# The first group's lists and the first expert block moved ahead, and five later steps that change places, in an attention and mixture-of-experts kernel

## The chip, the cores and the metric

The kernel runs on one core of one Trainium2 chip. The metric is the device time of one execution in microseconds (us). The engines are TensorE (PE, with its weight loads as PEld), VectorE (DVE), ScalarE (ACT), GpSimd (POOL) and SyncE (SP). Each runs its own instructions in the order in which they are written. They meet only at semaphores, and all large loads and transpositions are DMAs that SP issues.

## The reference

Linear attention with positive random features, and a mixture of experts with one expert for each token on its result:

```
def phi(x):
    proj = np.einsum('bhsd,md->bhsm', x, omega)
    sq = np.sum(x * x, axis=-1, keepdims=True) / 2.0
    h = proj - sq
    h = h - np.max(h, axis=-1, keepdims=True)
    return np.exp(h) / np.sqrt(m)
q_p, k_p = phi(q * scale), phi(k * scale)
kv = np.einsum('bhsm,bhsd->bhmd', k_p, v);  z = np.sum(k_p, axis=2)
num = np.einsum('bhsm,bhmd->bhsd', q_p, kv)
den = np.einsum('bhsm,bhm->bhs', q_p, z)[..., None] + 1e-06
x = num / den                      # 8 batches, 8 heads, 576 tokens, 64 wide
...
logits = x @ w_gate                # 4608 tokens, 512 wide, 8 experts
e_idx = np.argmax(logits, axis=1)
...
for e in range(E):
    mask = e_idx == e
    h = np.maximum(x[mask] @ w1[e], 0.0)
    ye = h @ w2[e]
    out[mask] = gate_w[mask, None] * eom[mask, e, None] * ye
```

All of it is in float32; the kernel splits operands into a float16 high half and a float16 low half and adds products.

## The kernel before

The attention is cut into 32 units u (one head of two batches, 1152 positions of keys and of queries). The 32 units make four groups of eight units, and after each group the tokens of its two batches are routed: a chain of small DVE instructions finds expert and place of each token, and lists which tokens make up the blocks of 128 rows of one expert. Each block n is then worked: its rows are gathered, transposed, multiplied with the first weights (two halves, hA and hB), passed through relu, and multiplied with the second weights (out.n.0 and out.n.1). Blocks of one group run among the units of the next.

The order of all of this is one hand-written table of words, ORDER. Plan.order walks through it, and every word emits its instructions on its own engine, so that the table sets the order on each of the five engines. A second table, BANKS, gives each step that needs PSUM one of eight banks; a step that takes a bank waits until the step that had it before is done with it. A third, FILL, says how many matmuls of 512 columns each of six steps warm.0 to warm.5 issues; their results are thrown away. The words that matter here (for the halves of a unit, n = 2u is the key, n = 2u+1 the query):

- pp.u.g (L681, PE): projections of a third g of unit u, into one bank for the key and one for the query, 18 matmuls which alternate between the two; mx.n.g (L699, DVE) takes the extremum of one bank, nb.u.g (L706, L710, DVE) makes the bias of both, and ex.n.g (L716, ACT, three exponentials) empties one bank.
- eh.n (L737, ACT) and el.n (L739, POOL): the high and the low half of the exponentials of n; eT.u (L781, SP): the transposition of the query's halves by DMA; pn.u.0 and pn.u.5 (L867, L874, PE) read its result; xf.u (L881 to L885, DVE) divides.
- kv.u.0 and kv.u.1 (L804, from unit 12 on L798, PE): the sums of key features times values; then one after another kvs.u (L824, DVE), kt.u (L840, PE), ke.u (L849, ACT), kg.u (L846, PE), gh.u (L852, ACT) and gl.u (L855, DVE), which releases the bank of kv.
- lists.g, pid.g, gi.g, controls.g: the end of a group's routing. lists.g (L1172 to L1183, DVE) feeds pid.g (L1306, PE), and that gi.g (L1313, L1339, DVE), the addresses for the gathers gx.n (L1584, POOL). xt.n (L1595, SP) transposes what gx.n gathered.
- w0h and w0l (L521 on ACT, L526 on DVE): halves of the first expert's weights; sw.n.1 and sw.n.2: on ACT and DVE, a branch that splits new weights if block n has another expert than the one before. hA.n and hB.n (L1618, PE) wait for xt.n and for sw.n.1 on both engines; relu.n (L1625, ACT) and rest.n (L1629, DVE) follow; out.n (L1651, PE) waits for rest.n and sw.n.2; os.n (L1694, ACT) and put.n (POOL) write the result.
- lga.u (L920, POOL) adds unit u's part of the gates' logits; lo.u (L591, POOL) makes the low half of unit u's input.

A gather gx.n in this table carries a mark such as gx.0<9: it also waits until the transposition eT.9 has landed.

Of the kernel before, what the change touches and what calls it, by code (L numbers as in the profile page):

```python
# [113 lines left out]
bounded.0 eh.21 gl.9 xf.8.0 mx.22.0 advance.0:0 ld.t.13 xf.8.5:0 pp.11.1 flag.0.1.ACT+DVE mx.23.0 w0h.2.3 advance.0:1 mx.22.1 pn.9.5 xf.9.5:0 w0h.2.2
advance.0:2 gx.2<9 xt.0 mx.23.1 nb.11.0:0 kv.10.0 el.21 xf.8.5:1 nb.11.1:0 advance.0:3 xf.9.5:1 nb.11.0 w0h.1.3 nb.11.1 advance.0:4 kv.10.1 ex.22.1
ld.t.14 xf.8.5 eT.10 kvh.10 advance.0:5 xf.9.5 w0l.1.3 pn.9.0 kvs.10 xf.9.0:0 w0l.1.2 flag.0.1.SP ex.23.0 pp.11.2 ex.23.1 xf.9.0:1 bring.0.1 ex.22.0
kt.10 advance.0:6 sw.0.1 hi.13.0 pp.12.0 xf.9.0 bring.1.1 advance.0:7 mx.24.0 w0h.2.1 advance.0:8 lo.13.0 warm.3 hA.0 mx.22.2 ke.10 sqr.12 w0h.2.0
mx.25.0 mx.23.2 relu.0.0 advance.0:9 nb.12.0:0 nb.11.2:0 kg.10 advance.0:10 nb.12.0 nb.11.2 ld.v.12 lga.8 w0l.2.1 gx.1<9 hB.0 gh.10 gl.10 rest.0.0
ex.22.2 ex.23.2 w0l.2.2 w0l.2.3 sqa.13 relu.0.1 kv.11.0 ex.24.0 pp.12.1 advance.0 kv.11.1 pp.12.2 w0l.2.0 bring.0.2 sw.0.2 eh.23 mx.24.1 out.0.0
ex.25.0 sw.1.1 el.23 mx.24.2 ld.t.15 xh.8 mx.25.1 nb.12.1:0 ld.n.15 hi.14.0 bring.2.1 kvh.11 pn.10.5 nb.12.1 mx.25.2 ld.n.14 vh.12 ld.v.13 xt.1 eT.11  # L120
rest.0.1 bring.1.2 nb.12.2:0 xl.8 ex.25.1 xf.10.5:0 ex.24.1 nb.12.2 sqr.13 vl.12 out.0.1 pn.10.0 ex.24.2 ex.25.2 xf.10.5:1 sqa.14 xf.10.5 pp.13.0
eh.24 os.0 lo.14.0 kvs.11 sw.1.2 mx.26.0 hA.1 eh.25 kt.11 mx.27.0 ke.11 pp.13.1 ld.v.14 xf.10.0:0 xf.10.0:1 nb.13.0:0 relu.1.0 hB.1 el.24 sqr.14
xf.10.0 kg.11 nb.13.0 xh.9 mx.26.1 ex.26.0 rest.1.0 ld.n.16 mx.27.1 kv.12.0 nb.13.1:0 el.25 nb.13.1 ex.27.0 sw.2.1 sqa.15 pp.13.2 ld.t.16 mx.26.2
ex.27.1 mx.27.2 nb.13.2:0 out.1.0 gh.11 xt.2 eT.12 ex.26.1 relu.1.1 vh.13 gl.11 nb.13.2 pp.14.0 ld.n.17 bring.2.2 ex.27.2 rest.1.1 ex.26.2 sqr.15
mx.28.0 kv.12.1 sqa.16 kvh.12 eh.26 mx.29.0 hi.15.0 lga.9 kvs.12 pn.11.0 pp.14.1 mx.28.1 out.1.1 nb.14.0:0 eh.27 nb.14.0 gx.3<11 xl.9 vl.13 mx.29.1
nb.14.1:0 ex.28.0 put.0<11 bring.3.1 kt.12 el.26 xf.11.0:0 os.1 hA.2 xh.10 rows.4 sqr.16 ex.29.0 nb.14.1 pn.11.5 ex.29.1 xt.3 pp.14.2 ex.28.1 kv.13.0
xf.11.5:0 sw.2.2 ke.12 mx.28.2 lga.10 xf.11.0:1 xf.11.5:1 kg.12 hi.16.0 hB.2 xf.11.5 mx.29.2 gh.12 sw.3.1 nb.14.2:0 gl.12 lo.15.0 nb.14.2 relu.2.0
ld.v.15 ex.28.2 ld.n.18 pn.12.5 ex.29.2 rest.2.0 kv.13.1 relu.2.1 ld.t.17 vh.14 kvh.13 pn.12.0 pp.15.0 el.27 eh.28 kvs.13 eT.13 kt.13 sqa.17 vh.15
xl.10 hA.3 xf.12.5:0 gx.4<12 mx.30.0 ke.13 mx.31.0 kg.13 vl.14 xf.11.0 sqr.17 gh.13 xf.12.0:0 xf.12.0:1 xf.12.5:1 gl.13 xh.11 eh.29 xf.12.0 out.2.0
# [1660 lines left out]
```

## Time and profile before

| | |
|---|---|
| median of 3 runs | 623.45 us (618.49 to 624.92) |
| the profiled execution | 623.36 us, its span 621.6 us |
| PE busy | 587.6 us, 95% of the span |
| ACT busy, DVE busy, POOL busy | 413.9, 408.0, 361.2 us |
| mean granted TensorE clock | 0.996 of full speed |

How to read it: PE is busy nearly all the time, so that in most places a microsecond counts only if PE waits in it. Busy time does not tell useful work from thrown-away work (warm) and does not tell where PE waits; both are read from the timeline of one engine, where a merged row gives start, length, engine, line, operation and operands, the number of instructions, and in brackets how long the engine stood idle before and who released it.

### The profile page before, as it was taken

What the parts mean: (1) busy time and instruction counts of PE and PEld (TensorE: products, weight loads), DVE (VectorE), ACT (ScalarE), POOL (GpSimd) and SP (SyncE); (2) the same over time, 40 slices, a digit from 0 to 9 for tenths busy, and PEclk for the clock granted to TensorE, in tenths of its full rate; (3) what the DMA queues carried; (4) which work ended last, traced back from release to release, by engine and by line L of the source; (5) the groups of instructions that cost most, each with busy time, mean ns of one, the idle gap of its engine ahead of it and who ended that gap; (6) DMA issues with size and microseconds to landing.
All of it is one profiled execution on the core that took longest, in us unless ns stands there. A gap on an engine that the chain in (4) does not pass through costs nothing. (4 is left out here: it accounts for less than half of the span.)

```text
span 621.6 us, 21399 instructions
## 1 busy us (share of the span) xinstructions
PE 587.6 (95%) x8442; PEld 451.1 (73%) x8442; DVE 408.0 (66%) x1114; ACT 413.9 (67%) x971; POOL 361.2 (58%) x265
## 2 busy tenths in 40 slices
...
GB/s 296 274 291 293 314 269 195 246 268 246 346 208 247 213 215 263 194 197 245 285 236 247 145 203 204 150 227 221 184 147 338 93 91 132 295 65 91 109 289 33
DMA packets 144686, 133.74 MB, mean 215 GB/s; under 512 B 104606, under 2 KB 124448, under 8 KB 143264
## 3 DMA queue, kind: packets, MB, share of 16 engines
...
q8 instruction: 82, 1.34, 0.9%
q14 instruction: 60, 0.49, 0.3%
...
## 5 line engine op out<-in xcount | busy, mean ns | idle before, releaser
L716 ACT ACTIVATE ef<-pp,nb 128x128 f32<-128x128 f32 x576 | 164.6, 393 | 40.2 <-DVE nb L710 29.6
L699 DVE TENSOR_REDUCE pp<-pp 128x3 f32<-128x384 f32 x192 | 106.7, 562 | 46.6 <-PE pp L681 40.6
L739 POOL TENSOR_TENSOR es<-ef,es 128x1152 f16<-128x1152 f32 x44 | 104.5, 2378 | 38.4 <-ACT es L737 21.7
L1618 PE MATMUL ph<-xt,w1h 128*128 128x128 f16 (+1 forms) x2048 | 122.2, 217 | 1.0 <-issue 0.6
L1618 PEld LDWEIGHTS <-w1h 128*128 128x128 f16 x2048 | 113.5, 98 | 6.9 <-issue 1.7
L1584 POOL DMA_INDIRECT gx<-rows,gi x38 | 41.0, 1079 | 130.1 <-ACTq L1551 63.3
L1629 DVE SCALAR_TENSOR_TENSOR hl<-ph,hh 128x512 f16<-128x512 f32 (+1 forms) x76 | 50.6, 666 | 99.7 <-ACTq L1551 73.8
L1651 PEld LDWEIGHTS <-hh 128*128 128x128 f16 x560 | 51.5, 98 | 54.5 <-issue 0.8
L1625 ACT ACTIVATE hh<-ph 128x512 f16<-128x512 f32 (+1 forms) x76 | 44.7, 591 | 65.6 <-PE ph L1618 50.9
L1618 PE MATMUL ph<-xt,w1l 128*128 128x128 f16 (+1 forms) x1024 | 66.7, 218 | 2.3 <-issue 2.3
L591 POOL TENSOR_TENSOR xlo<-xt,xhi 128x1152 f16<-128x1152 f32 x24 | 57.2, 2381 | 11.2 <-ACT xhi L588 11.1
L1651 PE MATMUL po<-w2h,hh 128*128 128x512 f16 x240 | 62.6, 383 | 0.0
L1651 PE MATMUL po<-w2h,hl 128*128 128x512 f16 x240 | 62.3, 382 | 0.0
L1651 PE MATMUL po<-w2l,hh 128*128 128x512 f16 x240 | 61.6, 379 | 0.0
L1694 ACT ACTIVATE os<-po,gx 128x512 f32<-128x512 f32 (+1 forms) x35 | 24.2, 692 | 54.9 <-PE po L1651 45.6
L1618 PEld LDWEIGHTS <-w1l 128*128 128x128 f16 x1024 | 58.5, 98 | 2.8 <-issue 2.8
L737 ACT CAST es<-ef 128x1152 f16<-128x1152 f32 x44 | 51.6, 1178 | 4.4 <-DMA et<-es 3.5
L1651 PEld LDWEIGHTS <-hl 128*128 128x128 f16 x280 | 27.5, 99 | 33.9 <-issue 1.1
L907 POOL TENSOR_TENSOR xs<-xf,xs 128x576 f16<-128x576 f32 x32 | 40.9, 1281 | 17.4 <-DVE nb L710 6.6
L867 PE MATMUL pn<-kvs,et 128*128 128x81 f16 x768 | 39.9, 201 | 3.1 <-DMA et<-es 1.2
L867 PEld LDWEIGHTS <-et 128*128 128x128 f16 x768 | 34.3, 97 | 8.7 <-issue 3.1
L681 PEld LDWEIGHTS <-xhi 64*128 64x128 f16 x864 | 25.6, 94 | 15.7 <-issue 9.0
...
## 6 DMA issues: line engine op xcount, KB each, us to landing
...
```

What stands on the lines that cost most here:

```text
L591: plan.add(("lo", u, x), ("POOL",), lambda t0=t0, t1=t1: nc.gpsimd.tensor_tensor(out=xl(u)[:, t0:t1], in0=xt32(u)[:, t0:t1], in1=xh(u)[:, ...
L699: nc.vector.tensor_reduce(out=spare(g, 0)[:, i], in_=banks["pp", 2 * u + i, g][:, 0:3, :], op=ALU.min, axis=AX.X)
L716: nc.scalar.activation(ef(2 * u + i)[:, c, :], banks["pp", 2 * u + i, g][:, c % 3, :], AF.Exp, bias=nb(u)[:, i, c : c + 1], scale=-SK)
L737: nc.scalar.copy(es(slot_es(n))[:, 0], ef(n))
L739: nc.gpsimd.tensor_tensor(out=es(slot_es(n))[:, 1], in0=ef(n), in1=es(slot_es(n))[:, 0], op=ALU.subtract)
L867: nc.tensor.matmul(pn[:, c - c0, :], a[:, c, :], w[:, :, 0 if c < 4 else 1], start=(i == 0 and c == c0), stop=(c == NC - 1 and i == len(op ...
L907: nc.gpsimd.tensor_tensor(out=x[:, :, P + o : P + o + D], in0=xf(u)[:, :, 0:D], in1=x[:, :, o : o + D], op=ALU.subtract)
L1584: return nc.gpsimd.indirect_dma_start(out=gx(n), out_offset=None, in_=rows[0 : (j + 1) * NC * P], in_offset=bass.IndirectOffsetOnAxis(ap=t ...
L1618: nc.tensor.matmul(ph[:, f4, 0:w_], w[qd][:, kk, fo : fo + P], xt(n)[:, x, 0:w_], start=(z == 0 and f4 == 0 and x == 0), stop=(z == 1 and ...
L1625: nc.scalar.activation(hh(n)[:, sl, 0:w_], banks["ph", n, g][:, :, 0:w_], AF.Relu)
L1629: nc.vector.scalar_tensor_tensor(out=hl(n)[:, sl, 0:w_], in0=banks["ph", n, g][:, :, 0:w_], scalar=0.0, in1=hh(n)[:, sl, 0:w_], op0=ALU.ma ...
L1651: nc.tensor.matmul(po, x(n)[:, f, :], w[f // 2][:, f % 2, :], start=(f == 0 and a == 0), stop=(f == FC - 1 and a == 2))
```

## The change

No arithmetic is added or removed, but for four matmuls of FILL whose results nobody reads: warm.2 goes from 8 to 7 and warm.3 from 4 to 1. Everything else is order:

1. Around the first group's routing (units 8 to 13): lists.0, pid.0, gi.0 and the gather gx.0 go ahead of mx.21.2 and of the bias of unit 10's last third; mx.20.2 goes behind lists.0, and four links of controls.0 go behind gi.0. On POOL gx.0 goes ahead of lo.12.0, on SP xt.0 ahead of two loads (ld.v.11, ld.t.13). On PE pid.0 goes ahead of pn.8.0 and warm.5, warm.3 ahead of pn.9.0, and hA.0 ahead of kt.10 and pp.12.0. On ACT w0h.1.3 goes ahead of two others, ex.22.0 ahead of four steps, and ex.21.1 and ex.21.2 swap. On DVE sw.0.1 goes ahead of one link of advance.0. Three banks of PSUM change hands: warm.5, pid.0 and pn.8.5.
2. On ACT eh.41 goes behind relu.9.0, ex.43.1 and ex.43.2; on POOL el.41 behind vl.21.
3. On ACT eh.48 goes behind ex.49.2 and ex.49.1.
4. On PE kv.24.0 goes behind hB.14.
5. On ACT ex.53.1 goes ahead of os.14.
6. On POOL el.63 goes ahead of lga.29.

The core of the diff (one line of the first region, one of the second edit, and the end of FILL; the other lines are words of the table in another order):

```
-pn.8.5 kg.9 ex.21.2 ex.21.1 gi.0:0 pp.11.0 lo.12.0 controls.0:3 ld.v.10 xf.8.0:0 gi.0 ex.20.2 ld.v.11 controls.0 xf.8.0:1 w0l.1.0 gh.9 gx.0<9
...
+lists.0:0 ke.9 lists.0:1 warm.2 sqa.12 lists.0 pid.0 mx.20.2 gi.0:0 gi.0 gx.0<9 lo.12.0 mx.21.2 nb.10.2:0 gl.8 pn.8.0 warm.5 controls.0:0 nb.10.2
...
+xf.9.0:1 bring.0.1 sw.0.1 hA.0 kt.10 advance.0:6 hi.13.0 pp.12.0 xf.9.0 bring.1.1 advance.0:7 mx.24.0 w0h.2.1 advance.0:8 lo.13.0 mx.22.2 ke.10 sqr.12
...
-relu.9.0 el.41 pn.19.0 kvh.20 vl.21 ex.43.1 rest.9.0 ex.43.2 pp.22.0 kvs.20 xf.19.0:0 sw.10.1 ex.42.2 eh.42 mx.44.0 relu.9.1 kt.20 el.42 advance.1:4
...
-FILL = (5, 6, 8, 4, 4, 3,)
+FILL = (5, 6, 7, 1, 4, 3,)
```

Three places of it, engine by engine. First PE around the first block, before (kv_2049 is unit 10's bank, pp_0_2179 and pp_0_2180 those of pp.12.0, ph_0 that of hA.0, ph_1 that of hB.0; of runs that alternate one row stands for each kind):

```order
L681 MATMUL pp_2_2127<-omh,xlo_1830 128x128
...
L840 MATMUL kv_2049<-cmt,kvs_2078 128x128
L681 MATMUL pp_0_2179<-omh,xhi_1823 128x128
...
L681 MATMUL pp_0_2180<-omh,xlo_1949 128x128
L479 MATMUL fill_2219<-omh 128x512
L1618 MATMUL ph_0_2224<-xt_2044,w1h_85 128x128
...
L846 MATMUL kv_2049<-wgh,kvf_2274 128x32
L1618 MATMUL ph_1_2300<-xt_2044,w1h_87 128x128
```

And now:

```order
L681 MATMUL pp_2_2131<-omh,xlo_1830 128x128
...
L1618 MATMUL ph_0_2175<-xt_2040,w1h_85 128x128
...
L840 MATMUL kv_2049<-cmt,kvs_2080 128x128
L681 MATMUL pp_0_2229<-omh,xhi_1823 128x128
...
L681 MATMUL pp_0_2230<-omh,xlo_1876 128x128
L846 MATMUL kv_2049<-wgh,kvf_2270 128x32
L1618 MATMUL ph_1_2296<-xt_2040,w1h_87 128x128
```

The first half of the first block now stands directly behind pp.11.2, and unit 10's kt and the whole of pp.12.0 stand behind it; the filling matmuls are gone from here.

Second DVE at the end of the first group's routing, before (r_itc is what lists.0 makes, pid what PE made of it, gi the addresses, pp_2 the banks of unit 10's last third, w1l a low half of weights):

```order
L699 TENSOR_REDUCE pp_2_1802<-pp_2_1802 128x3
...
L1079 TENSOR_TENSOR place<-cmt,rt_1605 128x1152
...
L699 TENSOR_REDUCE pp_2_1802<-pp_2_1803 128x3
...
L1183 TENSOR_TENSOR r_itc<-r_eq,rt_1605 128x18x8
L526 SCALAR_TENSOR_TENSOR w1l_90<-r_101,w1h_86 128x1024
L1313 TENSOR_REDUCE pid_1895<-pid_1895 128x8
...
L1339 CAST gi_1957<-pid_1895 128x8
```

And now:

```order
L1079 TENSOR_TENSOR place<-cmt,rt_1605 128x1152
...
L1183 TENSOR_TENSOR r_itc<-r_eq,rt_1605 128x18x8
L699 TENSOR_REDUCE pp_2_1802<-pp_2_1802 128x3
L1313 TENSOR_REDUCE pid_1860<-pid_1860 128x8
L1339 CAST gi_1872<-pid_1860 128x8
L699 TENSOR_REDUCE pp_2_1802<-pp_2_1803 128x3
...
L526 SCALAR_TENSOR_TENSOR w1l_90<-r_101,w1h_86 128x1024
```

One reduction alone stands now between lists.0 and the two links that wait for PE's answer, where a reduction's bias, controls and a split of weights stood.

Third POOL at the end of the attention, before (es_10433 is unit 31's query, lga the sum of logits, xs the rows that unit 29 writes):

```order
L1584 DMA gx_10448<-rows,gi_8234 128x528
...
L920 TENSOR_TENSOR lga_8995<-lga_8995,xf_10230 128x144
L739 TENSOR_TENSOR es_10433<-ef_10061,es_10433 128x1152
L907 TENSOR_TENSOR xs_10193<-xf_10230,xs_10193 128x9x64
```

And now:

```order
L1584 DMA gx_10444<-rows,gi_8230 128x528
...
L739 TENSOR_TENSOR es_10429<-ef_10057,es_10429 128x1152
L920 TENSOR_TENSOR lga_8991<-lga_8991,xf_10226 128x144
L907 TENSOR_TENSOR xs_10189<-xf_10226,xs_10189 128x9x64
```

The low half of unit 31 no longer stands behind a sum that waits for unit 29's division.

## Rows read from the trace of the kernel before

**Rows 1.** Busy time by stretch: stretch, its length, each engine, clock, DMA, GB/s.

```profile
100.00:150.00 50.00, 48.26 (x778) 38.66 (x777) 41.88 (x117) 47.55 (x117) 35.09 (x23) 1.00 1.02 255
```

**Rows 2.** Timeline of PE around the first block.

```profile
108.30 0.27 PE L840 MATMUL kv<-cmt,kvs 128*128 128x128 f16 x2 [0.60 <-DVE den L881]
...
108.91 0.36 PE L681 MATMUL pp<-omh,xlo 64*128 64x128 f16 x6
109.39 1.02 PE L479 MATMUL fill<-omh 128*128 128x512 f16 x4
110.47 1.95 PE L1618 MATMUL ph<-xt,w1h 128*128 128x128 f16 x32
...
113.15 0.18 PE L846 MATMUL kv<-wgh,kvf 128*128 128x32 f16 x1
...
115.90 1.34 PE L804 MATMUL kv<-rawv,ef 128*128 128x130 f32 x10
```

**Rows 3.** Timeline of DVE there.

```profile
105.51 0.20 DVE L710 SCALAR_TENSOR_TENSOR nb<-pp,sqs 128x6 f32<-128x6 f32 x2
...
110.34 0.56 DVE L699 TENSOR_REDUCE pp<-pp 128x3 f32<-128x384 f32 x1
...
115.14 0.20 DVE L855 SCALAR_TENSOR_TENSOR kvs<-kv,kvs 128x32 f16<-128x32 f32 x1
```

**Rows 4.** Timeline of ACT there.

```profile
109.54 1.15 ACT L588 CAST xhi<-xt 128x1152 f16<-128x1152 f32 x1 [0.20 <-ACTq L1546]
```

**Rows 5.** Timeline of POOL there.

```profile
101.23 2.03 POOL L1584 DMA_INDIRECT gx<-rows,gi  x1 [2.10 <-DVE den L883]
```

**Rows 6.** Timeline of DVE in the third group's routing, two links of one chain.

```profile
339.12 0.24 DVE L1137 TENSOR_TENSOR rt<-cft,rt 128x72 f32<-128x72 f32 x1
339.39 0.23 DVE L1139 TENSOR_TENSOR r_within<-rt,r_avs 128x72 f32<-128x72 f32 x1
```

**Rows 7.** Timeline of ACT at unit 20's query.

```profile
256.06 1.15 ACT L737 CAST es<-ef 128x1152 f16<-128x1152 f32 x1 [1.92 <-DMA et<-es]
```

**Rows 8.** Timeline of PE at the same place.

```profile
258.54 0.21 PE L681 MATMUL pp<-omh,xhi 64*128 64x128 f16 x1 [0.32 <-ACT ef L716]
259.31 0.33 PE L681 MATMUL pp<-omh,xhi 64*128 64x128 f16 x5 [0.56 <-ACTq L1546]
```

**Rows 9.** Timeline of ACT at unit 24's key.

```profile
315.26 0.37 ACT L849 CAST kvf<-kv 128x256 f16<-128x256 f32 x1 [0.17 <-ACTq L1546]
```

**Rows 10.** Timeline of PE at units 24 and 25.

```profile
315.74 0.19 PE L846 MATMUL kv<-wgh,kvf 128*128 128x32 f16 x1
...
331.66 0.77 PE L798 MATMUL kv<-vs,es 128*128 128x65 f16 x20 [0.62 <-ACT ef L716]
```

**Rows 11.** Timeline of ACT at block 14's result.

```profile
348.53 0.69 ACT L1694 ACTIVATE os<-po,gx 128x512 f32<-128x512 f32 x1 [3.72 <-PE kv L846]
349.12 0.88 ACT L716 ACTIVATE ef<-pp,nb 128x128 f32<-128x128 f32 x3
```

**Rows 12.** Timeline of PE at the same place.

```profile
350.04 0.32 PE L681 MATMUL pp<-omh,xhi 64*128 64x128 f16 x5 [1.45 <-ACT ef L716]
```

**Rows 13.** Timelines of ACT, POOL and SP at unit 31's query.

```profile
431.50 1.15 ACT L737 CAST es<-ef 128x1152 f16<-128x1152 f32 x1
...
436.00 0.49 POOL L920 TENSOR_TENSOR lga<-lga,xf 128x144 f32<-128x144 f32 x1 [3.44 <-DVE xf L885]
436.45 2.38 POOL L739 TENSOR_TENSOR es<-ef,es 128x1152 f16<-128x1152 f32 x1
...
438.85 2.75 SPq L781 DMA_TRANSPOSE et<-es  x1
```

**Rows 14.** Timeline of PE where it reads that transposition.

```profile
445.41 1.09 PE L867 MATMUL pn<-kvs,et 128*128 128x81 f16 x24 [1.22 <-DMA et<-es]
```

**Rows 15.** Timeline of PE, and busy time by stretch, where the clock fell.

```profile
479.18 0.80 PE L1618 MATMUL ph<-xt,w1l 128*128 128x128 f16 x8 [1.06 <-issue]
...
480.00:490.00 10.00, 9.46 (x110) 5.32 (x109) 6.26 (x8) 5.68 (x7) 1.99 (x2) 0.86 0.62 110
```

More of the change, by code (lines that the diff above doesn't have):

```diff
@@ L110 @@
 kt.8 weigh.0:1 nb.10.0 assign.0:0 nb.10.1:0 weigh.0:2 w0h.1.1 ex.20.0 assign.0:1 kvh.9 weigh.0 nb.10.1 assign.0:2 ke.8 ex.20.1 places.0:0 scales.0
-assign.0:3 places.0:1 warm.1 kg.8 pp.10.2 assign.0:4 hi.12.0 ex.21.0 kvs.9 lo.11.0 assign.0:5 kt.9 mx.20.2 gh.8 assign.0:6 w0h.1.2 places.0 assign.0
-eT.9 mx.21.2 controls.0:0 lists.0:0 ke.9 nb.10.2:0 gl.8 controls.0:1 lists.0:1 controls.0:2 warm.2 pn.8.0 nb.10.2 sqa.12 lists.0 warm.5 pid.0 w0l.1.1
-pn.8.5 kg.9 ex.21.2 ex.21.1 gi.0:0 pp.11.0 lo.12.0 controls.0:3 ld.v.10 xf.8.0:0 gi.0 ex.20.2 ld.v.11 controls.0 xf.8.0:1 w0l.1.0 gh.9 gx.0<9
@@ L114 @@
[L114 to L129, printed above, removed]
@@ L130 @@
-bring.4.1 xf.12.5 rest.2.1 pp.15.1 nb.15.0:0 lo.16.0 el.28 sqa.18 kv.14.0 mx.30.1 bring.3.2 vl.15 out.2.1 nb.15.0 xt.4 mx.31.1 ex.30.0 nb.15.1:0
-sw.3.2 xl.11 el.29 bring.4.2 sqr.18 pn.13.0 nb.15.1 ex.31.0 ex.31.1 relu.3.0 rest.3.0 ld.v.16 put.1<12 pp.15.2 lga.11 ld.n.19 kv.14.1 xh.12 hi.17.0
-mx.30.2 hB.3 mx.31.2 xf.13.0:0 nb.15.2:0 nb.15.2 xf.13.0:1 kvh.14 eT.14 xl.12 ex.30.1 kvs.14 ex.31.2 xf.13.0 relu.3.1 pn.13.5 xf.13.5:0 lga.12
+assign.0:3 places.0:1 warm.1 kg.8 pp.10.2 assign.0:4 hi.12.0 ex.21.0 kvs.9 lo.11.0 assign.0:5 kt.9 gh.8 assign.0:6 w0h.1.2 places.0 assign.0 eT.9
@@ new lines @@
+lists.0:0 ke.9 lists.0:1 warm.2 sqa.12 lists.0 pid.0 mx.20.2 gi.0:0 gi.0 gx.0<9 lo.12.0 mx.21.2 nb.10.2:0 gl.8 pn.8.0 warm.5 controls.0:0 nb.10.2
+controls.0:1 controls.0:2 controls.0:3 w0l.1.1 pn.8.5 kg.9 ex.21.1 ex.21.2 pp.11.0 ld.v.10 xf.8.0:0 ex.20.2 controls.0 xf.8.0:1 w0l.1.0 gh.9 bounded.0
+eh.21 gl.9 xf.8.0 mx.22.0 advance.0:0 xf.8.5:0 pp.11.1 flag.0.1.ACT+DVE mx.23.0 w0h.1.3 w0h.2.3 advance.0:1 mx.22.1 pn.9.5 xf.9.5:0 w0h.2.2
+advance.0:2 gx.2<9 xt.0 ld.v.11 ld.t.13 mx.23.1 nb.11.0:0 kv.10.0 el.21 xf.8.5:1 nb.11.1:0 advance.0:3 xf.9.5:1 nb.11.0 nb.11.1 advance.0:4 kv.10.1
@@ new lines @@
+ex.22.0 ex.22.1 ld.t.14 xf.8.5 eT.10 kvh.10 advance.0:5 xf.9.5 w0l.1.3 warm.3 pn.9.0 kvs.10 xf.9.0:0 w0l.1.2 flag.0.1.SP ex.23.0 pp.11.2 ex.23.1
+xf.9.0:1 bring.0.1 sw.0.1 hA.0 kt.10 advance.0:6 hi.13.0 pp.12.0 xf.9.0 bring.1.1 advance.0:7 mx.24.0 w0h.2.1 advance.0:8 lo.13.0 mx.22.2 ke.10 sqr.12
+w0h.2.0 mx.25.0 mx.23.2 relu.0.0 advance.0:9 nb.12.0:0 nb.11.2:0 kg.10 advance.0:10 nb.12.0 nb.11.2 ld.v.12 lga.8 w0l.2.1 gx.1<9 hB.0 gh.10 gl.10
+rest.0.0 ex.22.2 ex.23.2 w0l.2.2 w0l.2.3 sqa.13 relu.0.1 kv.11.0 ex.24.0 pp.12.1 advance.0 kv.11.1 pp.12.2 w0l.2.0 bring.0.2 sw.0.2 eh.23 mx.24.1
@@ new lines @@
+out.0.0 ex.25.0 sw.1.1 el.23 mx.24.2 ld.t.15 xh.8 mx.25.1 nb.12.1:0 ld.n.15 hi.14.0 bring.2.1 kvh.11 pn.10.5 nb.12.1 mx.25.2 ld.n.14 vh.12 ld.v.13
+xt.1 eT.11 rest.0.1 bring.1.2 nb.12.2:0 xl.8 ex.25.1 xf.10.5:0 ex.24.1 nb.12.2 sqr.13 vl.12 out.0.1 pn.10.0 ex.24.2 ex.25.2 xf.10.5:1 sqa.14 xf.10.5
+pp.13.0 eh.24 os.0 lo.14.0 kvs.11 sw.1.2 mx.26.0 hA.1 eh.25 kt.11 mx.27.0 ke.11 pp.13.1 ld.v.14 xf.10.0:0 xf.10.0:1 nb.13.0:0 relu.1.0 hB.1 el.24
+sqr.14 xf.10.0 kg.11 nb.13.0 xh.9 mx.26.1 ex.26.0 rest.1.0 ld.n.16 mx.27.1 kv.12.0 nb.13.1:0 el.25 nb.13.1 ex.27.0 sw.2.1 sqa.15 pp.13.2 ld.t.16
@@ new lines @@
+mx.26.2 ex.27.1 mx.27.2 nb.13.2:0 out.1.0 gh.11 xt.2 eT.12 ex.26.1 relu.1.1 vh.13 gl.11 nb.13.2 pp.14.0 ld.n.17 bring.2.2 ex.27.2 rest.1.1 ex.26.2
+sqr.15 mx.28.0 kv.12.1 sqa.16 kvh.12 eh.26 mx.29.0 hi.15.0 lga.9 kvs.12 pn.11.0 pp.14.1 mx.28.1 out.1.1 nb.14.0:0 eh.27 nb.14.0 gx.3<11 xl.9 vl.13
+mx.29.1 nb.14.1:0 ex.28.0 put.0<11 bring.3.1 kt.12 el.26 xf.11.0:0 os.1 hA.2 xh.10 rows.4 sqr.16 ex.29.0 nb.14.1 pn.11.5 ex.29.1 xt.3 pp.14.2 ex.28.1
+kv.13.0 xf.11.5:0 sw.2.2 ke.12 mx.28.2 lga.10 xf.11.0:1 xf.11.5:1 kg.12 hi.16.0 hB.2 xf.11.5 mx.29.2 gh.12 sw.3.1 nb.14.2:0 gl.12 lo.15.0 nb.14.2
@@ new lines @@
+relu.2.0 ld.v.15 ex.28.2 ld.n.18 pn.12.5 ex.29.2 rest.2.0 kv.13.1 relu.2.1 ld.t.17 vh.14 kvh.13 pn.12.0 pp.15.0 el.27 eh.28 kvs.13 eT.13 kt.13 sqa.17
+vh.15 xl.10 hA.3 xf.12.5:0 gx.4<12 mx.30.0 ke.13 mx.31.0 kg.13 vl.14 xf.11.0 sqr.17 gh.13 xf.12.0:0 xf.12.0:1 xf.12.5:1 gl.13 xh.11 eh.29 xf.12.0
+out.2.0 bring.4.1 xf.12.5 rest.2.1 pp.15.1 nb.15.0:0 lo.16.0 el.28 sqa.18 kv.14.0 mx.30.1 bring.3.2 vl.15 out.2.1 nb.15.0 xt.4 mx.31.1 ex.30.0
+nb.15.1:0 sw.3.2 xl.11 el.29 bring.4.2 sqr.18 pn.13.0 nb.15.1 ex.31.0 ex.31.1 relu.3.0 rest.3.0 ld.v.16 put.1<12 pp.15.2 lga.11 ld.n.19 kv.14.1 xh.12
@@ L133 @@
+hi.17.0 mx.30.2 hB.3 mx.31.2 xf.13.0:0 nb.15.2:0 nb.15.2 xf.13.0:1 kvh.14 eT.14 xl.12 ex.30.1 kvs.14 ex.31.2 xf.13.0 relu.3.1 pn.13.5 xf.13.5:0 lga.12
 rest.3.1 kt.14 out.3.0 ke.14 sw.4.1 xf.13.5:1 xf.13.5 pp.16.0 os.2 ex.30.2 out.3.1 sw.4.2 hA.4 relu.4.0 pp.16.1 ld.t.18 kg.14 rest.4.0 mx.32.1 mx.32.0
```

17 lines of the change are left out of this document (9 added, 8 removed).

## The prediction

> **What bounds the kernel now.** I read the page's engine shares first, then the busy time by stretch, then the timelines of single engines at each place that the diff touches. PE is busy in nearly all of the span, and after the first block starts it hardly stops: from 100 to 150 us it works 48.26 of 50 us, and ACT 47.55 of 50 beside it [rows 1]. So a microsecond counts where PE waits, and a moved step is worth what it takes from or adds to such a wait. The reader is to see in the PE rows the brackets, which say how long PE stood and for whom. There are four kinds of them here: PE waits for a bank that an exponential on ACT has not emptied [rows 8, 10, 12], for a transposition that has not landed [rows 14], for DVE [rows 2], and it is kept going by four filling matmuls in the same group, which are waits in disguise.
>
> **The first block: the lists and the gather.** lists.0 moves ahead of two reductions of DVE and pid.0 ahead of pn.8.0 on PE; that brings gi.0, and with it gx.0, earlier by about 1.4 us at most. The price lies on DVE: small instructions that stood between other work now follow what they depend on. Two instructions without dependence take 0.20 us together [rows 3]; two links of one chain start 0.27 us apart though one takes 0.24 [rows 6]. That is some 0.12 us more for a dependent neighbour. I count six new ones (assign's last but one link, two of lists, gi, one bias, controls), which makes 0.7 us, with a short wait for pid.0 inside it. I take DVE 0.7 us later from here on; the bounds are nothing (the links hide as before) and 1.1 us (one full wait for PE on top). On POOL lo.12.0 falls behind gx.0 [rows 5], which itself stands until its addresses and eT.9 are there. What needs lo.12.0 is pp.12.0, which comes eight microseconds later even in the old order, so this costs nothing; without that distance it would cost gx.0's 2.03 us. On SP the loads of unit 13's input and unit 11's values now wait behind xt.0, so behind gx.0's landing; their first reader is hi.13.0 at 109.54 [rows 4]. I cost that at nothing, with up to a microsecond on ACT if they are late.
>
> **The first block: hA.0 ahead of kt.10 and pp.12.0.** This is the term that I expect to go against the change. Before, PE did kt.10 and pp.12.0 from 108.30 to 109.27, four fills, and began hA.0 at 110.47 without standing idle [rows 2]. hA.0 needs sw.0.1 on ACT and on DVE, and ACT passed it just before the row that starts at 109.54 [rows 4]. Nothing was taken from ACT's queue ahead of it, so hA.0 cannot start before some 109.4. With ex.22.0 now ahead on ACT and waiting for a bias that ends at 105.71 [rows 3] plus DVE's 0.7, ACT is some 0.6 us later too: hA.0 starts near 110.05, 0.4 us earlier than before. It takes 113.15 - 110.47 = 2.68 us, and kt.10 with pp.12.0 takes 0.97 [rows 2], so pp.12.0 ends near 113.7 instead of 109.3. DVE is at mx.24.0, which reads it, and was there at 110.34 [rows 3]: it stands for about 2.7 us beside its own 0.7, and all behind it on DVE comes 3.35 us later, the biases that ACT's next exponentials need and gl.10 among them. gl.10 ended at 115.34 [rows 3] and now ends near 118.7. It releases the bank that kv.11.0 takes. kv.11.0 began at 115.90 on a PE that had no gap [rows 2]; it now begins near 118.7. PE has hB.0 to do until about 116.4 and then stands. **Loss: 2.8 us.** The four fewer fills (4 x 0.215 from the 1.02 us of four with its tail [rows 2], 0.86 us) are already inside, since PE waits where they stood. Bounds: if DVE and ACT are not late at all, mx.24.0 waits until 113.05 and the loss is 2.1; if DVE is 1.1 late and its queue slips further, 3.6. Between them I stay near the middle. PE has almost no slack afterwards [rows 1], so the loss is not given back.
>
> The clock speaks to the same place. At 479.18 PE had stood 1.06 us, after two shorter gaps, and in the ten microseconds from 480 the mean granted clock was 0.86 [rows 15]: the level of 1.2 GHz for a part of it, worth 1.4 us of full-speed time. At 445.41 it had stood 1.22 us [rows 14], and no fall shows. The Trainium skill, in TensorE: Matmul & The Clock Gate, section Part 1: The HAM clock gate, says that the array's clock halves when the array has been idle and comes back only after sustained work; the trace agrees for the first of these places and not for the second, and by that page alone the sum would be some 1.4 us more, 624.1 us.
>
> **Unit 20's high half (edit 2).** eh.41 held ACT for 1.92 us until a transposition had read its buffer, and for its own 1.15 us [rows 7], with relu.9.0 and two exponentials behind it. PE waited for these two: 0.32 and 0.56 us [rows 8]. In front of it they come 1.1 us earlier or more, and both waits go: **0.9 us gained**. el.41 and eT.20 come 1.4 us later; pn.20.0 reads them more than ten microseconds on, which covers it. Bounds 0.5 to 1.0.
>
> **Unit 24's high half (edit 3).** The two exponentials behind eh.48 come some 1.1 us earlier, and pp.25.0 no longer waits for their banks. But kg.23 behind it started at 315.74 [rows 10], 0.11 us after ke.23 ended on ACT (315.26 + 0.37 [rows 9]), and ke.23 stays behind the same work. PE waits for ke.23 instead: **0.1 us**, bounds 0 and 0.5 (what a faster bias brings later).
>
> **Unit 24's sums (edit 4).** kv.24.0 made PE wait 0.62 us for its bank [rows 10]. hB.14 does not need that bank and takes the place: **0.6 us**, bounds 0.3 and 0.7.
>
> **Unit 26's exponential (edit 5).** The second matmul of pp.26.2 waited 1.45 us for ex.53.1 [rows 12], which stood behind os.14: 349.12 - 348.53 = 0.59 us earlier [rows 11]. **0.6 us**, bounds 0.4 and 0.6; the rest of the wait stays, as ACT is not free before.
>
> **Unit 31's low half (edit 6).** lga.29 kept POOL standing 3.44 us for unit 29's division, with el.63 behind it [rows 13], though eh.63 was done at 432.65. el.63 can start 3.8 us earlier than 436.45, and eT.31 with it. It was issued at 438.85 and PE stood 1.22 us for it [rows 14]. With 3.8 us in hand the wait goes whole: **1.2 us**, bounds 0.6 (loads slow the transposition) and 1.3. Unit 31 ends the attention, so the last routing comes earlier by the same. lga.29 still starts when its data is there.
>
> **The sum.** Against the profiled execution's 623.36 us: + 2.8 - 0.9 - 0.1 - 0.6 - 0.6 - 1.2 = **622.8 us**, a hair under the median of the runs shown, 623.45. With the bounds: + 3.6 - 1.8 gives 625.2, + 2.1 - 4.1 gives 621.4.
>
> **The rivals.** (a) The first block costs nothing: DVE's wait for pp.12.0 is covered, because PE's next steps need nothing that DVE does there, and the fills' 0.86 us is a gain. For it speaks that PE waits openly only 0.60 us in that stretch [rows 2]; against it, that gl.10 releases kv.11.0's bank. Then 623.36 - 3.4 - 0.86 = 619.1 us. (b) The clock falls after the new waits at hA.0 and kv.11.0, together over 3 us of standing with no fills in them. It decides if the granted clock is under 1.00 between 110 and 125 us. Price 1.4 us for one fall [rows 15]: 624.2 us, slower than before. For it speaks row 479.18; against it, that PE works between the two waits for six microseconds. (c) The gains of edits 2 to 6 are taken by the next wait on the same engine, as I expect of edit 3 alone: half of 3.4 is lost, and 622.8 + 1.7 = 624.5 us.
>
> **How the numbers follow.** Forecast 0.50, (a) 0.20, (b) 0.15, (c) 0.15. The likeliest time is 622.8. The range takes in (a) below and (c) with the bounds above, 619.0 to 626.3; the runs shown spread over six microseconds, which I count as covered by these ends. A measurement of this kernel tells about 1% from no change, 6.2 us. No case goes that far either way: faster 0.04, within 1% 0.93, slower 0.03 for what the cases leave out.
>
> **What would show it.** Right: hA.0 near 110 on PE, pp.12.0 directly behind it, one long wait of DVE ahead of mx.24.0, PE standing two microseconds ahead of kv.11.0; later no wait of PE at pp.22.0, kv.24.0 and pn.31.5, a shorter one at pp.26.2, and one ahead of kg.23. Wrong: DVE without that wait, a block that starts before 109.4, a clock under 1.00 near 115 us, or a wait for eT.31 that stays. If the waits at edits 2 to 6 go and PE's lead at 450 us is not the sum of them, work that I took for covered was not.

## The result, and the profile after

The change makes the kernel slower: 629.49 us (median of 11 runs) against 622.67 us of the kernel before beside it, a ratio of 1.0106 (95% interval 1.0072 to 1.0140). 622.8 us were forecast, and 619.0 to 626.3 as the range; the time lies outside. The profiled execution of the changed kernel has a span of 629.5 us.

Where the time goes is read from the starts of PE's steps in both traces, each counted from the start of kt.9 (95.60 us before, 97.05 after; the 1.45 us between these two come from the first 25 us, where nothing is changed). "Late" is after minus before:

| PE step | late, us | what lies between |
|---|---|---|
| pn.8.0 | 0.77 | pid.0 ahead of it |
| pn.9.5 | 4.01 | PE waits in pp.11.1, just ahead, for a bank that bounded.0 frees (DVE, L1345) |
| kv.11.0 | 6.43 | hA.0 ahead of pp.12.0 |
| pp.13.0 | 6.92 | the first block is done |
| pn.19.0, kt.20 | 7.56, 6.41 | 0.6 lost at out.7.0, where nothing is changed; then edit 2 gains 1.15 |
| kg.23 | 7.04 | edit 3 |
| kv.24.1 | 6.84 | 0.5 gained at pp.26.0, where nothing is changed; 0.1 lost at edit 4 |
| kt.25 | 5.19 | edit 5 gains 1.65 |
| hA.21 | 6.02 | 0.63 lost again at pp.27.0, 0.2 at kv.29.0 |
| kt.31 | 8.46 | edit 6: a new wait of 2.45 |
| pn.31.5 | 7.08 | edit 6: eT.31 is there |

So the first block costs 6.9 us where 2.8 were forecast, and edits 2 to 6 together give nothing where 3.4 were. PE around the first block in the changed kernel, the answer to [rows 2] (timeline: start, length, engine, line, operation, operands, count, and in brackets the idle time before and who ended it):

```profile
99.73 0.39 PE L1306 MATMUL pid<-r_itc,place 128*128 128x16 f16 x9 [0.90 <-DVE r_itc L1183]
...
101.79 0.43 PE L867 MATMUL pn<-kvs,et 128*128 128x81 f16 x4 [1.35 <-DVE kvs L855]
...
107.84 0.32 PE L681 MATMUL pp<-omh,xhi 64*128 64x128 f16 x5 [2.01 <-DVE oi L1345]
...
115.03 1.96 PE L1618 MATMUL ph<-xt,w1h 128*128 128x128 f16 x32 [0.45 <-ACTq L1546]
...
123.78 1.39 PE L804 MATMUL kv<-rawv,ef 128*128 128x130 f32 x10 [2.31 <-DVE kvs L855]
```

The last row is the wait ahead of kv.11.0 that was forecast. The third, two microseconds for DVE, was not: the second bank of pp.11.1 is the one that pid.0 had, and bounded.0 on DVE (L1345) frees it. Its cause is on DVE and POOL, the answers to [rows 3, 5]; DVE first:

```profile
102.13 4.19 DVE L526 SCALAR_TENSOR_TENSOR w1l<-r,w1h 128x1024 f16<-128x1024 f32 x1
106.24 0.15 DVE L881 TENSOR_SCALAR den<-pn 128x5 f32<-128x5 f32 x1
...
107.63 0.16 DVE L1345 TENSOR_TENSOR oi<-pid,r_none 128x8 uint32<-128x8 f32 x1
107.70 0.19 DVE L855 SCALAR_TENSOR_TENSOR kvs<-kv,kvs 128x32 f16<-128x32 f32 x1
...
118.71 0.57 DVE L699 TENSOR_REDUCE pp<-pp 128x3 f32<-128x384 f32 x1 [2.36 <-PE pp L681]
```

And POOL in the same stretch, gx.0 and then lo.12.0:

```profile
101.63 1.18 POOL L1584 DMA_INDIRECT gx<-rows,gi  x1 [3.91 <-DVE pp L699]
102.84 2.38 POOL L591 TENSOR_TENSOR xlo<-xt,xhi 128x1152 f16<-128x1152 f32 x1
```

The row of 4.19 us is w0l.1.1, one split of weights: DVE subtracts the high half (w1h) from the weights (r) and writes the low half (w1l). In the kernel before, the same two instructions, lo.12.0 and then w0l.1.1, did not meet:

```profile
96.75 2.37 POOL L591 TENSOR_TENSOR xlo<-xt,xhi 128x1152 f16<-128x1152 f32 x1 [0.50 <-ACT xhi L588]
...
99.18 1.23 DVE L526 SCALAR_TENSOR_TENSOR w1l<-r,w1h 128x1024 f16<-128x1024 f32 x1
```

There the split began 0.05 us behind lo.12.0's end. In the changed kernel lo.12.0 runs beside it, and it ends 1.09 us behind lo.12.0's end (102.84 + 2.38 = 105.22). gl.9 (L855) comes 4.0 us later than before, counted from kt.9, and 3.0 of these are this split's. The row of 118.71 is mx.24.0, whose wait of 2.36 us was forecast with 2.7.

The clock, by stretch (columns: length; busy us of PE, PEld, DVE, ACT, POOL; granted clock, DMA share, GB/s):

```profile
101.00:102.00 1.00, 0.21 (x4) 0.20 (x3) 0.96 (x7) 1.00 (x5) 0.37 (x1) 0.91 0.50 193
102.00:103.00 1.00, 1.00 (x12) 0.51 (x10) 1.00 (x4) 1.00 (x5) 0.97 (x2) 0.50 0.00 0
...
110.00:111.00 1.00, 1.00 (x7) 1.00 (x6) 1.00 (x10) 0.94 (x1) 0.00 (x0) 0.50 0.96 340
...
114.00:115.00 1.00, 0.59 (x18) 0.41 (x18) 0.97 (x2) 0.93 (x4) 0.00 (x0) 1.00 1.08 179
```

It fell to 0.50, the level of 1.2 GHz, after PE had stood 0.90 and 1.35 us, and again after the 2.01 us; behind the long waits at hA.0 and kv.11.0 it stayed at 1.00.

At the end of the attention the same thing is there. POOL's el.63, DVE's fourth split of block 21's w1l with gl.30 behind it, and PE at kt.31 and pn.31.5 (the last answers to [rows 14]):

```profile
440.43 2.37 POOL L739 TENSOR_TENSOR es<-ef,es 128x1152 f16<-128x1152 f32 x1 [1.29 <-ACT es L737]
...
440.46 3.42 DVE L526 SCALAR_TENSOR_TENSOR w1l<-r,w1h 128x1024 f16<-128x1024 f32 x1
443.80 0.19 DVE L855 SCALAR_TENSOR_TENSOR kvs<-kv,kvs 128x32 f16<-128x32 f32 x1
...
444.59 0.27 PE L840 MATMUL kv<-cmt,kvs 128*128 128x128 f16 x2 [2.45 <-DVE den L881]
...
453.94 1.08 PE L867 MATMUL pn<-kvs,et 128*128 128x81 f16 x24
```

eT.31 is in time now, as forecast. But el.63 began 0.03 us ahead of the split, the split ended 1.08 us behind it, and PE stood 2.45 us for what DVE does next.

### The profile page after: what moved, and what is told of

Its sections match the earlier page's. It is cut to its first block, busy times and chain, and to the rows that moved or that the text cites. A ratio compares the mean times of both kernels' runs of the same rounds, so it can differ in the third digit from the quotient of the medians.

```text
span 629.5 us, 21392 instructions
## 1 busy us (share of the span) xinstructions
PE 588.0 (93%) x8438; PEld 452.4 (72%) x8438; DVE 413.0 (66%) x1114; ACT 415.1 (66%) x971; POOL 361.9 (57%) x265
## 3 DMA queue, kind: packets, MB, share of 16 engines
q8 instruction: 82, 1.34, 0.9%
## 5 line engine op out<-in xcount | busy, mean ns | idle before, releaser
L1694 ACT ACTIVATE os<-po,gx 128x512 f32<-128x512 f32 (+1 forms) x35 | 24.1, 690 | 48.8 <-PE po L1651 47.9
L804 PE MATMUL kv<-rawv,ef 128*128 128x130 f32 x240 | 33.3, 288 | 2.8 <-DVE kvs L855 2.3
```

## The experiments

Ratios are against the kernel before on the same chip, which took 617.5 to 617.7 us there (runs 1 to 8 are of one chip, 9 to 12 of another). "Lost at pp.13.0" is the lateness of that step, counted from kt.9, against the second profile of before (below). Theory M: a split of weights on DVE that meets an elementwise instruction on POOL stands until POOL is done. Its rivals: C (the clock) and H (hA.0's place alone). The intervals of runs 1, 2, 3 and 8 overlap the changed kernel's 1.0072 to 1.0140, so that their times can't be told from it; what they show is read from the steps of one profile each. The times of runs 6 and 7 lie clear of each other.

**1. lo.12.0 back ahead of gx.0.**

```
-gi.0 gx.0<9 lo.12.0 mx.21.2
+gi.0 lo.12.0 gx.0<9 mx.21.2
```

> The changed kernel with one step moved: lo.12.0 again ahead of gx.0 on POOL. Theory M (a split of weights on DVE that meets a long POOL instruction stands until POOL is done): in the changed kernel w0l.1.1 took 4.19 us from 102.13 and ended 1.09 us behind lo.12.0; here it takes 1.2 us, gl.10 and kv.11.0 come some 3 us earlier against kt.9, and the time falls from 629.5 to about 626.5 us. Theory C (the clock): PE has stood the same 0.9 and 1.35 us ahead of w0l.1.1, so the clock falls all the same near 102 us, kv.10 still takes 3.8 us, and no more than 0.5 us comes back: 629 us. Theory H (hA.0 ahead of pp.12.0 alone is the loss): no change, 629.5 us.

Lost at pp.13.0: 4.02 us in place of 6.95. w0l.1.1:

```profile
100.50 1.18 POOL L1584 DMA_INDIRECT gx<-rows,gi  x1 [1.05 <-DVE pp L706]
...
101.00 1.22 DVE L526 SCALAR_TENSOR_TENSOR w1l<-r,w1h 128x1024 f16<-128x1024 f32 x1
```

The clock fell all the same (0.50 from 102 to 105 us), and yet 2.9 us came back, 2.3 of them up to pn.9.5: M, not C or H. The second fall of the changed kernel, at 108 us, went with the wait of 2.01 us ahead of it and has a part in the rest. Ratio 1.0085 (1.0054 to 1.0115).

**2. hA.0 back behind kt.10 and pp.12.0.**

```
-sw.0.1 hA.0 kt.10 advance.0:6 hi.13.0 pp.12.0
+sw.0.1 kt.10 advance.0:6 hi.13.0 pp.12.0 hA.0
```

> The changed kernel with hA.0 behind kt.10 and pp.12.0 again. Theory H, and the prediction's term: DVE's 2.36 us of standing ahead of mx.24.0 go and kv.11.0 starts 2.0 to 2.4 us earlier against kt.9; about 627.2 us. Theory M: the same amount and no more, since w0l.1.1 still takes 4.2 us; some 4.5 us of the first block's 6.9 stay. Theory C: nothing comes back before hA.0, and the long wait of PE ahead of kv.11.0 only moves: 629 us.

Lost at pp.13.0: 5.44, so 1.5 us came back and not 2.0 to 2.4. DVE no longer waits ahead of mx.24.0, but this execution had the clock at 0.50 from 102 to 112 us:

```profile
115.69 0.56 DVE L699 TENSOR_REDUCE pp<-pp 128x3 f32<-128x384 f32 x1
```

w0l.1.1 took 4.16 us again. Ratio 1.0096 (1.0067 to 1.0125).

**3. el.63 back behind lga.29** (`-el.63 lga.29`, `+lga.29 el.63`).

> The changed kernel with el.63 behind lga.29 again (edit 6 undone). Theory M: the fourth w1l split, 3.42 us in the changed kernel because it met el.63 by 0.03 us, takes 1.21 us; PE's 2.45 us of standing ahead of kt.31 go, the wait for eT.31 at pn.31.5 comes back with 1.2 to 1.4 us; net 1.0 us faster at pn.31.5 and 628.5 us in all. Rival (the 2.45 us come from lateness that DVE had collected before): kt.31 waits as before, the wait for eT.31 comes on top, and the time is some 1 us longer, 630.5 us.

The four splits took 5.26 us together, as before the change, and PE's wait ahead of kt.31 shrank to 0.26; the wait for eT.31 was back with 1.19:

```profile
438.68 0.27 PE L840 MATMUL kv<-cmt,kvs 128*128 128x128 f16 x2 [0.26 <-DVE den L881]
...
449.37 1.10 PE L867 MATMUL pn<-kvs,et 128*128 128x81 f16 x24 [1.19 <-DMA et<-es]
```

M again; the rival falls. The microsecond that it is worth is less than the total can show (1.0100, 1.0071 to 1.0129). This profile also speaks on C, as its first block is the changed kernel's: the clock stayed at 1.00 until 106 us, w0l.1.1 took 4.17 us all the same, and PE stood 3.29 us ahead of the second half of pp.11.1:

```profile
106.41 0.47 PE L681 MATMUL pp<-omh,xhi 64*128 64x128 f16 x5 [3.29 <-DVE oi L1345]
```

pn.9.5 came 4.38 us late, against 4.03 with the fall: what is lost up to there is not the clock's. Here it fell at 106 and again at 123 us, behind kv.11.0, and 7.8 us were lost at pp.13.0.

**4. Edits 2 to 5 on the kernel before** (the words of these four edits as in the change, all others as before).

> The kernel before with edits 2, 3, 4 and 5 alone. By the prediction's terms 0.9 + 0.1 + 0.6 + 0.6 = 2.2 us faster than before. By PE's stamps in the changed kernel: 1.15 (edit 2) + 0.25 behind it, 1.0 lost at pn.22.0 and kg.23 (edit 3 or a late load of weights), 0.44 (edit 4), 1.66 less 0.63 given back (edit 5): 1.9 us faster, 620.8 us. If the loss at kg.23 belongs to edit 3's order it is here too; if it was a load that edit 2 made late, it is here too but with the load late in the trace; if it was chance, it is gone and the kernel is 2.9 us faster, 619.8 us.

Ratio 1.0003 (0.9977 to 1.0029): no gain, a miss for every number expected. The next run shows why.

**5. The kernel before, once more** (no edit).

> The kernel before, profiled once more on the chip of the three kernels that follow, so that their stamps have a neighbour. Up to kt.31 its PE stamps should agree with the first profile to within 0.5 us, counted from kt.9; the stamps behind 470 us, where PE waits for weights and gathers, may differ by a microsecond or two.

A miss up to 5 us: the stamps agree to 0.05 us until 142 us, and then waits of the first profile are simply not there. eh.41 on ACT, where [rows 7] have a wait of 1.92 us, and PE at pp.22.0, where [rows 8] have 0.32 and 0.56:

```profile
252.68 1.19 ACT L737 CAST es<-ef 128x1152 f16<-128x1152 f32 x1
...
256.85 0.34 PE L681 MATMUL pp<-omh,xhi 64*128 64x128 f16 x6
```

In this execution pp.26.2 does not wait either (kt.25 comes 0.77 us behind pp.26.2's start, 2.26 before), and at pp.25.0 there is no wait as well. Edits 2 and 5 remove waits which one execution has and another has not. The two profiles of before are of times five microseconds apart (622.67 us in the median beside the first, 617.5 beside this one), but it is not a matter of the chip alone: run 6, on the same chip as this one, has eh.41 waiting again, and PE at pp.22.0 waiting 0.62 and 0.56 us:

```profile
262.15 1.15 ACT L737 CAST es<-ef 128x1152 f16<-128x1152 f32 x1 [2.23 <-DMA et<-es]
```

Against this profile the kernel with edits 2 to 5 is 0.9 us late at pn.29.5 and 0.2 us early at hB.27.

**6. The first block's edit alone, on the kernel before** (edits 2 to 6 taken out of the change).

> The kernel before with the first block's edit alone (lists, gather and hA.0 ahead; warm.2 and warm.3 cut), edits 2 to 6 left out. The prediction said 2.8 us lost; by PE's stamps in the changed kernel 6.9 us are lost at pp.13.0, of which 3.0 are DVE standing in w0l.1.1 behind lo.12.0, about 2 DVE waiting for pp.12.0, and about 2 the chain of lists. So about 6.9 us slower than before, ratio 1.011. If the first block were harmless and the later edits were the loss: ratio 1.00.

Ratio 1.0118 (1.0085 to 1.0150), lost at pp.13.0 6.95 us: the first block is the whole loss.

**7. Three steps back:** lo.12.0, hA.0 and el.63 as in 1, 2 and 3.

> The changed kernel with three steps put back: lo.12.0 ahead of gx.0, hA.0 behind pp.12.0, el.63 behind lga.29. Theory M and the order of hA.0 together: of the first block's 6.9 us at pp.13.0 some 5 go (3.0 and 2.0) and about 2 stay, which are the chain of lists; PE does not wait at kt.31; with the gains of edits 2, 4 and 5 of 1.1, 0.4 and 1.0 us the kernel ends level with before, ratio 0.999 to 1.002. Theory C (the clock falls because PE stands ahead of pid.0 and pn.8.0): the clock still falls near 102 us and 4 us or more stay at pp.13.0, ratio 1.005.

Ratio 1.0002 (0.9980 to 1.0024). Lost at pp.13.0: 0.92 us, less than the 2 expected. PE stood 0.91 and 1.34 us ahead of pid.0 and within pn.8.0, as in run 1 (0.90 and 1.34), and here the clock stayed at 1.00: the same standing brings a fall in one execution and none in another. The clock's column of run 1, then of this run:

```profile
102.00:103.00 1.00, 0.96 (x15) 0.95 (x14) 1.00 (x5) 0.50 (x2) 1.00 (x1) 0.50 0.62 118
...
102.00:103.00 1.00, 0.65 (x22) 0.48 (x16) 1.00 (x5) 1.00 (x2) 0.12 (x1) 1.00 0.64 173
```

**8. w0l.1.1 ahead of gi.0's two links**, lo.12.0 behind gx.0.

```
-gi.0:0 gi.0 gx.0<9 ... controls.0:3 w0l.1.1
+w0l.1.1 gi.0:0 gi.0 gx.0<9 ... controls.0:3
```

> The changed kernel with w0l.1.1 ahead of the two links of gi.0 on DVE, while POOL stands idle; lo.12.0 stays behind gx.0. Theory M: w0l.1.1 takes 1.2 us, gi.0 and gx.0 come some 0.8 us later, and of the 6.9 us at pp.13.0 about 2.2 go. Theory C: no more than 0.5 us go, since PE's standing ahead of gl.8 is there as before or longer. Rival to M (it is the order gx.0, lo.12.0 that costs, by gx.0's descriptors, and not the meeting with w0l.1.1): the 3 us stay, and another DVE instruction carries them.

Lost at pp.13.0: 6.01; one microsecond came back, not 2.2. w0l.1.1 took 1.21 us, but now the next split stood in its place; DVE, with lo.12.0 on POOL between:

```profile
98.02 1.21 DVE L526 SCALAR_TENSOR_TENSOR w1l<-r,w1h 128x1024 f16<-128x1024 f32 x1
...
101.22 2.38 POOL L591 TENSOR_TENSOR xlo<-xt,xhi 128x1152 f16<-128x1152 f32 x1
...
101.51 3.18 DVE L526 SCALAR_TENSOR_TENSOR w1l<-r,w1h 128x1024 f16<-128x1024 f32 x1
```

101.22 + 2.38 + 1.09 = 104.69, where the second split ends. My number missed because I had looked at one split only. That another DVE instruction carries the loss is what the rival said; its cause, gx.0's descriptors, does not hold: in run 1 w0l.1.1 ran beside gx.0 (the rows of run 1) and took 1.22 us. What this split and w0l.1.1 of the changed kernel have in common is the end, 1.09 us behind lo.12.0's. Ratio 1.0083 (1.0052 to 1.0114).

**9. Edit 6 alone, on the kernel before.**

> The kernel before with edit 6 alone (el.63 ahead of lga.29). The prediction: the wait for eT.31 goes, 1.2 us faster at pn.31.5. Theory M: el.63 starts within 0.1 us of the fourth split of w1l on DVE; where POOL is first by a hair the split takes 3.4 us, PE stands 2.4 us ahead of kt.31, the wait for eT.31 goes, and pn.31.5 comes 0.9 to 1.2 us later than before, ratio 1.001 to 1.002. If the two do not meet, kt.31 does not wait and the prediction's 1.2 us are gained.

Neither of the two amounts of M came: kt.31 did not wait, and from there pn.31.5 came 1.39 us earlier, which is the prediction's 1.2. The two instructions did meet, and POOL paid:

```profile
427.52 3.49 POOL L739 TENSOR_TENSOR es<-ef,es 128x1152 f16<-128x1152 f32 x1 [0.16 <-ACT es L737]
...
427.55 1.21 DVE L526 SCALAR_TENSOR_TENSOR w1l<-r,w1h 128x1024 f16<-128x1024 f32 x1
```

el.63 began 0.11 us before the third split ended, as it did, by 0.10 to 0.11 us, in the four executions where DVE paid (the changed kernel, runs 1, 2 and 8); there the fourth split took 3.41 or 3.42 us and el.63 2.37, here the split 1.21 and el.63 3.49. Which of them waits is not settled by the program's order, nor by anything that these timelines show. Ratio 1.0006 (0.9971 to 1.0040).

**10. Edit 6 with relu.20.1 ahead of eh.63 on ACT**, so that el.63 comes surely behind the split's start.

```
-eh.63 bring.21.2 ... kg.31 relu.20.1
+relu.20.1 eh.63 bring.21.2 ... kg.31
```

> Edit 6 on the kernel before, and on ACT relu.20.1, which was ready for seven microseconds, ahead of eh.63, so that el.63 starts some 0.5 us later and behind the start of the fourth split of w1l. Theory M: the split comes first and takes 1.2 us, el.63 runs behind it and ends some 2.5 us earlier than before, PE waits neither at kt.31 nor at pn.31.5, and pn.31.5 comes 1.2 to 1.6 us earlier than before, ratio 0.998. Rival (any POOL instruction beside the splits slows DVE, whoever is first): kt.31 waits 1 us or more as with edit 6 alone.

```profile
429.70 3.00 POOL L739 TENSOR_TENSOR es<-ef,es 128x1152 f16<-128x1152 f32 x1 [1.79 <-ACT es L737]
```

el.63 began 0.46 us behind the split's start and took 3.00 us; the split took 1.21, kt.31 did not wait, and from hA.21 to pn.31.5 PE needed 1.38 us less than in the second profile of before. The rival falls. Ratio 0.9983 (0.9958 to 1.0008), which can't be told from no change.

**11. Edits 2, 4, 5 and 10's pair of moves, on the kernel before.**

> The kernel before with edits 2, 4 and 5, edit 6, and relu.20.1 ahead of eh.63: what the traces leave of the change as a gain. If the waits that edits 2, 4 and 5 remove are there in this execution, 3 us faster than before; where they are not, as in the second profile of before, only the 1.2 to 1.6 us at eT.31 remain. Ratio 0.995 to 0.999.

Ratio 0.9982 (0.9958 to 1.0006): inside what was expected, and not measurably faster. Its profile is a miss: 2.6 us were lost up to hA.21 against the second profile of before, 0.6 of them at edit 4's place, and only 1.4 gained behind it.

**12. Run 2 with 11 filling matmuls in warm.2.**

> The changed kernel with hA.0 behind pp.12.0 again and with 11 filling matmuls in warm.2 in place of 7, so that PE does not stand ahead of pid.0. With 7 the clock fell near 101 us for ten microseconds and 5.4 us were lost at pp.13.0. If a fall of the clock is behind the part that neither the chain of lists (0.9) nor w0l.1.1 (3.0) explains, and the four matmuls prevent it, some 3.9 us are lost here, at a clock of 1.00; if the clock does not matter to the end, 5.4 us as before, whatever the clock does.

Lost at pp.13.0: 4.42, between the two. The fall came all the same, later and shorter: PE stood 3.30 us for bounded.0, which stands behind w0l.1.1 on DVE, and the clock was at 0.50 from 107 to 110 us, against 102 to 112 in run 2:

```profile
106.10 0.33 PE L681 MATMUL pp<-omh,xhi 64*128 64x128 f16 x5 [3.30 <-DVE oi L1345]
```

One microsecond for some seven fewer at 0.50; the clock counts, but as a follower of the waits.

## Why the prediction was wrong

**lo.12.0 behind gx.0 "costs nothing": the step that failed.** I asked who needs lo.12.0 (pp.12.0, late enough) and not what would run beside it at its new time. It fell onto w0l.1.1, which then took 4.19 us and not 1.2: 3.0 us (run 1: 2.93). The trace of before had such meetings. Three of its splits took longer than the others' 1.2 us, as this one of DVE's timeline in the kernel before, which met el.21 on POOL (104.53 to 106.93 us) and ended 1.09 us behind it:

```profile
106.57 1.46 DVE L526 SCALAR_TENSOR_TENSOR w1l<-r,w1h 128x1024 f16<-128x1024 f32 x1
```

In the fourteen traces of this case 41 of 784 splits took longer than 1.26 us, and all 41 ended 1.08 to 1.10 us behind the end of an elementwise POOL instruction that ran beside them. Splits and such instructions ran beside each other for more than 0.2 us 50 times; in the other nine the split took its 1.2 us, and POOL's instruction 2.77 to 3.49 us in place of 2.4, ending 2.23 to 2.25 us behind the split. So the section on the chip is wrong in one point: the engines do not meet only at semaphores. The Trainium skill has the rule, in SBUF — State Buffer, section Who interferes with whom: a VectorE instruction with two inputs in SBUF and a GpSimd instruction that reads SBUF share a port pair, and the one that comes second stands until the first is done. The traces agree for the splits, whose two inputs lie in SBUF. They agree as well for L1079, which reads one input from SBUF and the other from a bank of PSUM: it took 1.34 to 1.35 us beside POOL's work (42 times) and alone (14 times). No run here moved an input, so that the place of the inputs is the reason rests on that page and on these rows. Which of the two comes second can't be read from the recorded starts (below).

**hA.0 ahead of pp.12.0: right in place and size.** DVE waited 2.36 us ahead of mx.24.0 (2.70 in run 1) where 2.7 were forecast, and PE 2.31 us ahead of kv.11.0. gl.10 was forecast at 118.7 and ended at 123.72, which is 122.27 on the scale of the kernel before, since DVE had come 4.5 us late and not 0.7. For the same reason hA.0 began 3.1 us later than before and not 0.4 earlier.

**The chain of lists: right.** 0.7 us were forecast on DVE; with the other causes taken away 0.92 us are left (run 7). The parts 0.9 + 3.0 + 2.4 make 6.3 of the 6.95 us. The rest I put down to the clock, for which runs 2 and 12 differ by about a microsecond; an execution with all these waits and no fall there is none, so this part is not shown.

**Rival (b)** had a share in it, at another place: in the changed kernel's profile the clock fell ahead of the first block, where PE stood for lists.0, gl.8 and bounded.0 (so it was under 1.00 at 110 us, as (b) asks), and not after hA.0 and kv.11.0. In run 3, with the same first block, it fell behind kv.11.0, and from there to pp.13.0 some 1.1 us more were lost than in the changed kernel, where 1.4 were forecast. (The prediction's 624.1 and 624.2 for one fall are the same sum, 622.76 + 1.4.) **Rival (a)** is wrong: DVE's wait was not covered. **Rival (c)** comes nearest for edits 2 to 6: edits 3 and 4 lose theirs to a next wait of PE, the others for other reasons.

**Edits 2 and 5: a gain in one pair of profiles, none in another.** In the first pair edit 2 gave 1.15 us (0.9 forecast) and edit 5 1.65 (0.6), less 0.63 taken back at pp.27.0. The mechanism was right where the wait was there. The step that failed is the first one: to take a wait of one execution as one of the kernel. The second profile of before lacks these waits, and the timed ratio of edits 2 to 5 is 1.0003.

**Edit 3** gained 0.5 us at pp.25.0, and kg.23 then waited 0.92 us for ke.23, which had come later with a late load of weights; in run 4 the loss at kg.23 is there again, in runs 1 and 2 it is not. What sets this load's time was not tried. **Edit 4** gave nothing in the first pair. The step that failed is "hB.14 does not need that bank and takes the place": hB.14 has a bank of its own to wait for, that of out.13, which os.13 on ACT (L1694) frees. Before, os.13 ended at 332.19, just ahead of hB.14's start; in the changed kernel the wait has moved from kv.24.0 to hB.14 and is 0.71 us in place of 0.62. os.13 and hB.14 before, then after:

```profile
331.48 0.71 ACT L1694 ACTIVATE os<-po,gx 128x512 f32<-128x512 f32 x1
332.27 1.95 PE L1618 MATMUL ph<-xt,w1h 128*128 128x128 f16 x32
...
339.19 0.71 ACT L1694 ACTIVATE os<-po,gx 128x512 f32<-128x512 f32 x1
339.95 1.95 PE L1618 MATMUL ph<-xt,w1h 128*128 128x128 f16 x32 [0.71 <-ACT os L1694]
```

In runs 4, 7 and 11 it is 0.25, 0.85 and 1.20 us.

**Edit 6: the term was right and the sign open.** The wait for eT.31 goes, as forecast (1.2 us; 1.39 in run 9). "Work that I took for covered": el.63 in its new place meets a split, and in four executions DVE lost 2.2 us by it, in two (runs 9 and 12) POOL lost 1.1. Run 10, where POOL lost 0.6, keeps the gain and takes the chance out.
